# A fused attention and mixture-of-experts kernel: part of a weight conversion moved into the first expert, low parts of weights moved from GpSimd to VectorE

## The chip, the cores and the metric

One core of a Trainium2 chip. The metric is the device time of one execution, in microseconds. Engines: PE (TensorE), DVE (VectorE), ACT (ScalarE), POOL (GpSimd), SP (SyncE, which issues most of the loads here).

## What is computed

The reference, cut to what matters (x comes from the attention below; shapes in brackets):

```python
# attention with decay: B=4, H=8, S=768, D=64
state = gamma * state + einsum('bhd,bhe->bhde', k[:, :, t], v[:, :, t])
y[:, :, t] = scale * einsum('bhd,bhde->bhe', q[:, :, t], state)
# routing: x [3072, 512], w_gate [512, 8]; each expert takes 384 tokens
order = argsort(-(x @ w_gate).flatten())     # greedy, by falling logit
# experts: w1 [8, 512, 1024], w2 [8, 1024, 512]
out[mask_e] = maximum(x[mask_e] @ w1[e], 0) @ w2[e]
# dense block: w_in [512, 2048], w_out [2048, 512], both given in float64
h = x @ w_in
result = (maximum(h, 0) + log1p(exp(-abs(h)))) @ w_out
```

## The kernel before, in words

**Stages.** (1) Attention over 24 blocks of 128 tokens (class Attn), with the conversion of w_in and w_out laid beside it. (2) A gap in which only the routing of the first expert runs (Route.phase(0)). (3) Eight experts one after the other (class Ffn): for each, its 384 tokens are gathered from DRAM, go through w1, relu, w2 (steps M1 and M2, eight each), and then at once through the dense block (steps F1 and F2, sixteen each, on the same 384 columns); the rows are stored by an indirect DMA. The routing of the next expert runs beside the steps.

**Precision.** Every product of the experts is three matmuls in fp32r: high by high, low by high, high by low (mm3, lines 617 to 621). So every weight and every activation is split into a rounded high part (ACT, a copy into fp32r) and a low part, the difference. For weights this is split_w (lines 599 to 606): whi on ACT, wlo on POOL; w1, w2 and the rows of w_out are split each time they are used, 256 times in all. w_in is kept split (wih, wil). For activations it is split_act and split_g (lines 608 to 615, 688 to 698), low parts on DVE.

**Conversion.** w_in and w_out come as float64. Class Conv turns a piece of 128x512 into float32 with integer and float operations on DVE and one on ACT (line 240): operations m (line 233), cX (241), x (244), cX (247), e (251), F (260), and for w_in the low part (254). It is a generator: each yield is one step, and step() runs one. A piece of w_in takes seven, one of w_out six. It works on two pieces at once and loads raw pieces ahead (line 227). Attn.emit calls side(j, part) three times per block, which brings the steps done up to (3j + part) * 190 // 72: 187 of 208 by the end. The other 21 are run by fill() (line 833), one at each plain yield of Route.phase(0).

**Routing.** One phase picks one expert and its 384 tokens. top() finds each token's best expert still open, then a search in three levels counts tokens over thresholds: on DVE thr and G (compare, line 378), on PE 24 small matmuls (count, line 385), on DVE ind (431), on PE a sum over partitions (437), on DVE satj and base (440, 446). Then the expert is chosen (inc to ei, lines 466 to 474, mark "expert"), and its list of tokens is made (one-hots ohq, line 511; 24 matmuls, line 524; ix, line 529, mark "list"). Each yield ends a turn; what follows a yield is written to the queues later, after other work.

**Order.** All queues are in program order (manual_schedule). Ffn.plan lists the steps M1, M2, F1, F2 and transposes; Ffn.emit walks it. Before each step, weights(at + 4) makes sure that the split weights of the next four keys are written (ring of 6 pairs) and that raw loads are out ahead of them (4 buffers); then the step; then one turn of routing, at each step until the next expert's list is there, at every second step after that. Before F1 number 10 the next list is forced and its rows are gathered by POOL (fetch_x). fetch_w waits on SP for the number of the chosen expert.

Of the kernel before, what the change touches and what calls it, by code (L numbers as in the profile page):

```python
# [206 lines left out]
class Conv:  # L207
# [3 lines left out]
    def __init__(self, tc, ctx, W, plan):  # L211
        self.nc, self.W, self.plan = tc.nc, W, plan
        self.st = ctx.enter_context(tc.tile_pool(name="cst", bufs=2, side="right"))
        self.raw, self.loaded, self.ops = {}, 0, 0
        self.gen = self.run()

    def load(self, p):
        raw = self.raw[p] = self.st.tile([128, self.W, 2], I32, name="raw", bufs=3)
        self.nc.sync.dma_start(raw.rearrange("p n b -> p (n b)"), self.plan[p][0])

    def run(self):
# [4 lines left out]
        for p in range(N + 2):  # L226
            while self.loaded < min(p + 2, N):
                self.load(self.loaded)
                self.loaded += 1
# [27 lines left out]
            if b:  # L257
                to = self.plan[q][1]
                F = to[0] if len(to) == 1 else T("cF", FT, 2)
                v.tensor_tensor(F, m, e, op=OP.add)  # L260
                if len(to) == 2:
                    f = F.rearrange("p (a n) -> p a n", a=4)
                    nc.scalar.activation(to[0], f, AF.Copy)
                    c = f, to[1], to[0]
                yield
            b = a

    def step(self, to=None):

        while to is None or self.ops < to:  # L270
            self.ops += 1
            if next(self.gen, self) is self or to is None:
                return

# [6 lines left out]
class Route:  # L281
# [72 lines left out]
    def top(self, c0, c1, first):  # L354
# [5 lines left out]
        if not first:  # L360
            v.tensor_tensor(lm, src, self.pen[:, None, :].to_broadcast([128, n, E]), op=OP.add)
            src = lm
            v.tensor_scalar(self.u[:, s], self.asg[:, s], 0.0, None, op0=OP.is_equal)
        v.tensor_reduce(m, src, axis=AX.X, op=OP.max)
# [4 lines left out]
        v.tensor_reduce(aed, lm, axis=AX.X, op=OP.max)  # L369
        v.tensor_tensor(ik, m.bitcast(I32), sg, op=OP.bitwise_xor)  # L370
# [17 lines left out]
    def first_part(self, c0, c1):  # L388

        self.top(c0, c1, True)  # L390
        self.compare(c0, c1, self.t0, 46)

    def phase(self, i, slow=True):
# [5 lines left out]
        if i:  # L399
            self.top(0, N, False)  # L400
# [107 lines left out]
        h = N // 4  # L508
# [58 lines left out]
class Ffn:  # L567
# [7 lines left out]
    def open0(self, ctx):  # L575
        P = lambda name, bufs: ctx.enter_context(self.tc.tile_pool(name=name, bufs=bufs, reuse_waits="tile"))
        self.rawp = P("raw", 4)
        self.ring = P("ring", 6)
# [9 lines left out]
    def load_raw(self, key):  # L588
# [3 lines left out]
        raw = self.raws[key] = self.rawp.tile([128, 512], FT, name="wraw")  # L592
# [6 lines left out]
    def split_w(self, key):  # L599
        nc = self.nc  # L600
        raw = self.wout[key[2]] if key[0] == "wo" else self.raws.pop(key)
# [3 lines left out]
        nc.gpsimd.tensor_sub(lo, raw, hi.bitcast(FT))  # L605
# [161 lines left out]
    def emit(self):  # L767
# [9 lines left out]
        for n, (fn, i, f, key) in enumerate(G):  # L777
# [5 lines left out]
            fn(i, f)  # L783
            step += 1
# [3 lines left out]
    def weights(self, to):  # L788

        keys = self.keys  # L790
        while self.done < min(len(keys), to) and self.can(keys[self.done]):
            while self.loaded < min(len(keys), self.done + 4) and self.can(keys[self.loaded]):
                self.load_raw(keys[self.loaded])
                self.loaded += 1
# [21 lines left out]
    def start(self, fill):  # L816
# [5 lines left out]
        for mark in self.R.phase(0, False):  # L822
            self.marked(mark, 0)
            if mark == "expert":
                for k in self.keys[:4]:
# [6 lines left out]
            elif mark is None:  # L832
                fill()
# [10 lines left out]
def model(ctx, tc, qk, kv, w_gate, w1, w2, w_in, w_out, tab, gqt, out, B, H, S):  # L844
# [18 lines left out]
    cuts += [(w_out[f * 128:(f + 1) * 128], (wo[:, f],)) for f in range(16)]  # L863
# [3 lines left out]
    def side(j, part):  # L867
        cv.step((3 * j + part) * 190 // 72)
# [5 lines left out]
    a.emit(side, logits)  # L874
    c2.close()
    R.wp = ctx.enter_context(tc.tile_pool(name="rwork", bufs=1, reuse_waits="tile"))
# [3 lines left out]
    F.start(cv.step)  # L880
    cv.step(1000)
    c1.close()
    c0.close()
    F.open(ctx)
# [27 lines left out]
```

## Time and profile before

| | us |
|---|---|
| median of three runs | 1120.59 |
| the three runs | 1120.57, 1120.59, 1124.83 |
| the profiled execution | 1123.62 |
| its span, first to last instruction | 1121.5 |

| engine | busy us (share of the span) |
|---|---|
| PE | 1020.8 (91%) |
| DVE | 689.1 (61%) |
| ACT | 535.1 (48%) |
| POOL | 442.3 (39%) |

The shares are means over stages that differ: attention ends near 175 us, the first matmul of the first expert starts at 216.6, each expert takes 102 to 126 us. The mean granted TensorE clock is 0.957 of full speed. Matmuls are pipelined and their ends are modelled, so a busy PE in the tables need not be at its peak. Neighbouring operations of one engine overlap a little in the records, so sums of durations are some per cent above the busy time.

### The profile page before, as it was taken

What the parts mean: (1) busy time and instruction counts of PE and PEld (TensorE: products, weight loads), DVE (VectorE), ACT (ScalarE), POOL (GpSimd) and SP (SyncE); (2) the same over time, 40 slices, a digit from 0 to 9 for tenths busy, and PEclk for the clock granted to TensorE, in tenths of its full rate; (3) what the DMA queues carried; (4) which work ended last, traced back from release to release, by engine and by line L of the source; (5) the groups of instructions that cost most, each with busy time, mean ns of one, the idle gap of its engine ahead of it and who ended that gap; (6) DMA issues with size and microseconds to landing.
All of it is one profiled execution on the core that took longest, in us unless ns stands there. A gap on an engine that the chain in (4) does not pass through costs nothing.

```text
span 1121.5 us, 18513 instructions
## 1 busy us (share of the span) xinstructions
PE 1020.8 (91%) x7041; PEld 922.8 (82%) x7041; DVE 689.1 (61%) x1510; ACT 535.1 (48%) x1041; POOL 442.3 (39%) x386
## 2 busy tenths in 40 slices
PE   5877874489999999999999999999999999999997
PEld 5776763378878988898889888988888899989996
DVE  5999999755765656467646665865586622441332
ACT  2444332224554465436543654365536654664663
POOL 4323320333335424542355235523452454337422
PEclk9888886589999999999999999999999999999999
DMA  8887873320113201320122012301220222013000
GB/s 317 302 284 263 301 228 104 104 75 1 39 38 105 65 1 38 95 75 1 39 81 90 1 38 76 94 1 30 75 67 1 76 85 85 1 47 122 1 1 29
DMA packets 38873, 97.51 MB, mean 87 GB/s; under 512 B 5120, under 2 KB 5248, under 8 KB 38784
## 3 DMA queue, kind: packets, MB, share of 16 engines
q1 hardware_dynamic: 34128, 83.11, 23.1%
q0 software_dynamic: 3840, 12.59, 3.4%
q8 instruction: 55, 0.90, 0.3%
q10 hardware_dynamic: 816, 0.63, 0.2%
q14 instruction: 34, 0.28, 0.1%
HBM read 83.73 MB, written 12.58 MB: 86 GB/s over the span
## 4 chain that ended last, share of the span: by engine, by line
PE 68%; DVE 23%; issue 3%; ACT 2%; DMA 2%; POOL 1%; SPq 0%; ACTq 0%; POOLq 0%; DVEq 0%
PE h L619 11%; PE h L621 10%; PE h L620 10%; PE acc L717 8%; PE acc L719 7%; PE acc L718 7%; PE acc L619 3%; PE acc L621 3%; PE acc L620 3%; PE rt L385 2%; DVE at L121 2%; DVE cM L233 2%; DVE cX L247 2%; DVE cX L251 2%; DVE base L446 1%
## 5 line engine op out<-in xcount | busy, mean ns | idle before, releaser
L605 POOL TENSOR_TENSOR wlo<-wo,whi 128x512 fp32r<-128x512 f32 x128 | 169.2, 1327 | 357.9 <-ACT whi L604 325.4
L605 POOL TENSOR_TENSOR wlo<-wraw,whi 128x512 fp32r<-128x512 f32 x128 | 164.1, 1302 | 189.6 <-ACT whi L604 172.3
L683 DVE SCALAR_TENSOR_TENSOR gf<-h,sp 128x384 f32<-128x384 f32 x128 | 71.2, 557 | 179.0 <-ACT sp L681 178.9
L619 PE MATMUL h<-x2h,wih 128*128 128x384 f32 x512 | 176.8, 345 | 0.0
L621 PE MATMUL h<-x2l,wih 128*128 128x384 f32 x512 | 173.2, 338 | 0.2 <-DVE x2l L615 0.2
L620 PE MATMUL h<-x2h,wil 128*128 128x384 f32 x512 | 173.4, 339 | 0.0
L717 PE MATMUL acc<-whi,gh 128*128 128x512 f32 x384 | 154.8, 403 | 0.0
L719 PE MATMUL acc<-whi,gl 128*128 128x512 f32 x384 | 152.5, 397 | 2.2 <-DVE gl L697 2.2
L718 PE MATMUL acc<-wlo,gh 128*128 128x512 f32 x384 | 152.0, 396 | 0.0
L679 ACT ACTIVATE sp<-h 128x384 f32<-128x384 f32 x128 | 62.4, 488 | 150.3 <-PE h L621 148.9
L697 DVE TENSOR_TENSOR gl<-gf,gh 128x384 fp32r<-128x384 f32 x128 | 103.4, 807 | 39.9 <-ACT gh L696 39.8
L611 ACT ACTIVATE h1h<-h 128x384 fp32r<-128x384 f32 x64 | 31.4, 491 | 170.7 <-PE h L621 170.7
L612 DVE SCALAR_TENSOR_TENSOR h1l<-h,h1h 128x384 fp32r<-128x384 f32 x64 | 35.3, 555 | 115.6 <-ACT h1h L611 115.6
L619 PEld LDWEIGHTS h<-x2h,wih 128*128 128x128 f32 x512 | 96.1, 188 | 4.1
L620 PEld LDWEIGHTS h<-x2h,wil 128*128 128x128 f32 x512 | 96.2, 188 | 3.0
L621 PEld LDWEIGHTS h<-x2l,wih 128*128 128x128 f32 x512 | 96.1, 188 | 0.8 <-DVE x2l L615 0.8
L619 PE MATMUL acc<-h1h,whi 128*128 128x384 f32 x256 | 89.7, 350 | 0.0
L719 PEld LDWEIGHTS acc<-whi,gl 128*128 128x128 f32 x384 | 72.4, 189 | 21.0 <-DVE gl L697 4.3
L619 PE MATMUL h<-xh,whi 128*128 128x384 f32 x256 | 89.0, 348 | 0.7 <-ACT xh L614 0.7
L696 ACT ACTIVATE gh<-gf 128x384 fp32r<-128x384 f32 x128 | 67.1, 524 | 46.5 <-DVE gf L683 39.0
L621 PE MATMUL acc<-h1l,whi 128*128 128x384 f32 x256 | 87.4, 341 | 0.0
L620 PE MATMUL acc<-h1h,wlo 128*128 128x384 f32 x256 | 87.2, 341 | 0.0
(197 smaller groups left out, 2047.4 us busy)
## 6 DMA issues: line engine op xcount, KB each, us to landing
wraw<-in_moe_w_dram SPq DMA_DIRECT2D x128, 256.0 KB, 2.7
qk_t<-in_qk_dram SPq DMA_DIRECT2D x24, 512.0 KB, 6.8
kv_t<-in_kv_dram SPq DMA_DIRECT2D x24, 512.0 KB, 5.5
raw<-in_moe_w_in_dram SPq DMA_DIRECT2D x16, 512.0 KB, 5.3
raw<-in_moe_w_out_dram SPq DMA_DIRECT2D x16, 512.0 KB, 4.7
xd<-xs SPq DMA_DIRECT2D x24, 256.0 KB, 6.0
gqt<-in_gqt_dram SPq DMA_DIRECT2D x5, 256.0 KB, 6.6
ctab<-in_tab_dram ACTq DMA_DIRECT2D x1, 536.0 KB, 5.7
```

The lines of the kernel that those rows point to most:

```text
L605: nc.gpsimd.tensor_sub(lo, raw, hi.bitcast(FT))
L612: nc.vector.scalar_tensor_tensor(lo, ps, 0.0, hi.bitcast(FT), op0=OP.max, op1=OP.subtract)
L619: nc.tensor.matmul(ps, wh, ah, start=start, stop=False)
L620: nc.tensor.matmul(ps, wl, ah, start=False, stop=False)
L621: nc.tensor.matmul(ps, wh, al, start=False, stop=stop)
L679: nc.scalar.activation(a, ps, AF.Abs)
L683: nc.vector.scalar_tensor_tensor(g, ps, 0.0, a, op0=OP.max, op1=OP.add)
L696: nc.scalar.activation(gh, g, AF.Copy)
L697: nc.vector.tensor_tensor(gl, g, gh.bitcast(FT), op=OP.subtract)
L717: nc.tensor.matmul(ps, gh[:, s], wh, start=f == 0, stop=False)
L718: nc.tensor.matmul(ps, gh[:, s], wl, start=False, stop=False)
L719: nc.tensor.matmul(ps, gl[:, s], wh, start=False, stop=f == 15)
```

## The change

- Conv gets a number of raw buffers (bufs), counts the pieces it has made, and can be run until a given piece is done (until).
- In attention only w_in and the first 8 of the 16 rows of w_out are converted: 160 steps, spread so that the last call of side has done them all. Nothing of it is left for the gap: fill is gone.
- The other 8 rows are converted in the first expert, by a second Conv with pieces of 128x256 (16 of them, 96 steps): after each step of the plan with i == 0, three steps of it. split_w of a row of w_out first makes sure that its pieces are there.
- wlo is made on DVE (tensor_tensor) instead of POOL, in all 256 splits.
- A routing phase after the first has three more yields, two inside top() and one behind it.
- The ring has 5 pairs in place of 6, the raw weights 3 buffers in place of 4.

Cut to the changed lines and their neighbours:

```diff
@@ -208,14 +208,14 @@
-    def __init__(self, tc, ctx, W, plan):
-        self.nc, self.W, self.plan = tc.nc, W, plan
+    def __init__(self, tc, ctx, W, plan, bufs=3):
+        self.nc, self.W, self.plan, self.bufs = tc.nc, W, plan, bufs
         self.st = ctx.enter_context(tc.tile_pool(name="cst", bufs=2, side="right"))
-        self.raw, self.loaded, self.ops = {}, 0, 0
+        self.raw, self.loaded, self.ops, self.made = {}, 0, 0, 0
         self.gen = self.run()
     def load(self, p):
-        raw = self.raw[p] = self.st.tile([128, self.W, 2], I32, name="raw", bufs=3)
+        raw = self.raw[p] = self.st.tile([128, self.W, 2], I32, name="raw", bufs=self.bufs)
         self.nc.sync.dma_start(raw.rearrange("p n b -> p (n b)"), self.plan[p][0])
@@ -224,7 +224,7 @@
         for p in range(N + 2):
-            while self.loaded < min(p + 2, N):
+            while self.loaded < min(p + self.bufs - 1, N):
                 self.load(self.loaded)
@@ -262,6 +262,7 @@
                     c = f, to[1], to[0]
+                self.made += 1
                 yield
@@ -271,6 +272,10 @@
+    def until(self, made):
+        while self.made < min(made, len(self.plan)):
+            self.step()
@@ -361,12 +366,15 @@
             v.tensor_scalar(self.u[:, s], self.asg[:, s], 0.0, None, op0=OP.is_equal)
+            yield
         v.tensor_reduce(m, src, axis=AX.X, op=OP.max)
         v.tensor_reduce(aed, lm, axis=AX.X, op=OP.max)
+        if not first:
+            yield
         v.tensor_tensor(ik, m.bitcast(I32), sg, op=OP.bitwise_xor)
@@ -387,7 +395,8 @@
-        self.top(c0, c1, True)
+        for _ in self.top(c0, c1, True):
+            pass
         self.compare(c0, c1, self.t0, 46)
@@ -397,7 +406,8 @@
         if i:
-            self.top(0, N, False)
+            yield from self.top(0, N, False)
+            yield
         base = self.zero
@@ -575,7 +585,7 @@
         self.rawp = P("raw", 4)
-        self.ring = P("ring", 6)
+        self.ring = P("ring", 5)
@@ -589,7 +599,7 @@
             return
-        raw = self.raws[key] = self.rawp.tile([128, 512], FT, name="wraw")
+        raw = self.raws[key] = self.rawp.tile([128, 512], FT, name="wraw", bufs=3)
         e = bass.ds(self.regs[i], 1)
@@ -598,11 +608,13 @@
         nc = self.nc
+        if key[0] == "wo":
+            self.late.until(2 * (key[2] + 1 - self.kept))
         raw = self.wout[key[2]] if key[0] == "wo" else self.raws.pop(key)
         nc.scalar.activation(hi, raw, AF.Copy)
-        nc.gpsimd.tensor_sub(lo, raw, hi.bitcast(FT))
+        nc.vector.tensor_tensor(lo, raw, hi.bitcast(FT), op=OP.subtract)
         self.ws[key] = hi, lo
@@ -781,6 +793,9 @@
             fn(i, f)
+            if i == 0:
+                for _ in range(3):
+                    self.late.step()
             step += 1
@@ -789,7 +804,7 @@
         while self.done < min(len(keys), to) and self.can(keys[self.done]):
-            while self.loaded < min(len(keys), self.done + 4) and self.can(keys[self.loaded]):
+            while self.loaded < min(len(keys), self.done + 3) and self.can(keys[self.loaded]):
                 self.load_raw(keys[self.loaded])
@@ -813,7 +828,7 @@
-    def start(self, fill):
+    def start(self):
@@ -822,7 +837,7 @@
             if mark == "expert":
-                for k in self.keys[:4]:
+                for k in self.keys[:3]:
                     self.load_raw(k)
@@ -830,7 +845,6 @@
             elif mark is None:
-                fill()
                 if since is not None:
@@ -860,27 +874,32 @@
     cuts = [(w_in[f], (wih[:, :, f * 128:(f + 1) * 128], wil[:, :, f * 128:(f + 1) * 128])) for f in range(16)]
-    cuts += [(w_out[f * 128:(f + 1) * 128], (wo[:, f],)) for f in range(16)]
+    kept = 8
+    rows = [w_out[f * 128:(f + 1) * 128] for f in range(16)]
+    cuts += [(rows[f], (wo[:, f],)) for f in range(kept)]
     cv = Conv(tc, c1, 512, cuts)
     def side(j, part):
-        cv.step((3 * j + part) * 190 // 72)
+        cv.step((3 * j + part) * 162 // 71)
     a.emit(side, logits)
+    cv.step(1000)
     c2.close()
+    c1.close()
     R.wp = ctx.enter_context(tc.tile_pool(name="rwork", bufs=1, reuse_waits="tile"))
     F.open0(ctx)
-    F.start(cv.step)
-    cv.step(1000)
-    c1.close()
+    F.start()
     c0.close()
+    halves = [(rows[f][:, h * 512:h * 512 + 512], (wo[:, f, h * 256:h * 256 + 256],))
+              for f in range(kept, 16) for h in range(2)]
+    F.late, F.kept = Conv(tc, ctx, 256, halves, 3), kept
     F.open(ctx)
```

## Rows read from the trace of the kernel before

**Rows 1.** The page's chain of work that ended last, by engine, as shares of the span.
```profile
PE 68%; DVE 23%; issue 3%; ACT 2%; DMA 2%; POOL 1%; SPq 0%; ACTq 0%; POOLq 0%; DVEq 0%
```

**Rows 2.** Busy time of each engine by stage, us from the span's start: length, then PE, PEld (weight load), DVE, ACT, POOL busy us with instruction counts, the granted TensorE clock, the DMA engines' share and GB/s. Attention; the routing gap; a part of the gap with nearly the whole first routing phase; the first expert up to its first F1; the rest of the first expert; the later experts with routing beside them; an expert without.
```profile
18.00:175.50 157.50, 119.44 (x1370) 108.39 (x1370) 156.53 (x291) 66.07 (x131) 48.23 (x35) 0.88 0.81 272
175.50:216.60 41.10, 11.83 (x177) 9.00 (x173) 37.85 (x132) 6.80 (x11) 8.12 (x7) 0.55 0.36 107
178.30:211.30 33.00, 8.10 (x155) 6.50 (x154) 31.20 (x115) 3.86 (x6) 4.95 (x5) 0.52 0.26 82
216.60:268.30 51.70, 44.77 (x318) 41.48 (x318) 27.48 (x61) 13.24 (x27) 19.18 (x15) 0.86 0.14 43
268.30:335.50 67.20, 64.47 (x403) 56.83 (x403) 45.09 (x112) 37.16 (x73) 20.47 (x16) 0.97 0.11 32
335.50:907.50 572.00, 563.88 (x3606) 505.83 (x3606) 350.89 (x797) 294.02 (x573) 244.63 (x206) 1.00 0.17 52
907.50:1009.50 102.00, 102.00 (x542) 95.43 (x541) 33.54 (x49) 58.08 (x113) 47.09 (x41) 1.00 0.19 57
```

**Rows 3.** DVE's groups of instructions in attention (18 to 175.5 us), the six operations of a w_out piece: line, operation, tiles and shapes, count, busy us, mean ns of one, idle us before.
```profile
L233 DVE SCALAR_TENSOR_TENSOR cM<-cM,cX 128x512 f32<-128x512 f32 x29 | 24.8, 856 | 0.1
L247 DVE SCALAR_TENSOR_TENSOR cX<-raw,cX 128x512 int32<-128x512 int32 x29 | 21.8, 752 | 0.0
L251 DVE SCALAR_TENSOR_TENSOR cX<-raw,cX 128x512 f32<-128x512 uint32 x28 | 20.9, 747 | 0.0
L241 DVE TENSOR_SCALAR cX<-raw 128x512 int32<-128x512 int32 x29 | 16.6, 574 | 4.5 <-DMA raw<-in_moe_w_in_dram 4.5
L244 DVE TENSOR_SCALAR cX<-cM 128x512 int32<-128x512 int32 x28 | 15.5, 554 | 0.0
...
L260 DVE TENSOR_TENSOR wo<-cM,cX 128x512 f32<-128x512 f32 x12 | 10.8, 899 | 0.3
```

**Rows 4.** PE's groups in the same window, the one it waits before (idle us before it and what ended that).
```profile
L159 PE MATMUL pX<-rx,yT 128*128 128x136 f32 x184 | 32.2, 325 | 33.2 <-ACT yT L137 25.1 <-DVE cX L251 8.1
```

**Rows 5.** The timeline in the routing gap, one counting step of the first routing phase with the conversion steps beside it: start us, duration us, engine, line, operation, tiles; in brackets the engine's idle time before and what ended it.
```profile
186.53 1.08 PE L385 MATMUL pS<-G,oe 128*8 128x46 bf16 x24 [1.18 <-DVE G L378]
...
186.75 0.42 DVE L244 TENSOR_SCALAR cX<-cM 128x512 int32<-128x512 int32 x1
187.08 0.68 DVE L247 SCALAR_TENSOR_TENSOR cX<-raw,cX 128x512 int32<-128x512 int32 x1
...
187.68 0.25 DVE L431 TENSOR_SCALAR ind<-pS,r 8x46 bf16<-8x46 f32 x1
187.86 0.67 DVE L251 SCALAR_TENSOR_TENSOR cX<-raw,cX 128x512 f32<-128x512 uint32 x1
187.99 0.19 PE L437 MATMUL pS<-ind,ones 8*128 8x46 bf16 x1 [0.38 <-DVE ind L431]
...
188.46 0.19 DVE L440 SCALAR_TENSOR_TENSOR satj<-pS,st 128x46 bf16<-128x46 f32 x1
```

**Rows 6.** The same timeline from the first expert's choice to the making of its list.
```profile
196.33 0.17 PE L464 MATMUL pS<-rs,ones 128*128 128x8 bf16 x1 [1.82 <-DVE rs L457]
...
197.08 0.69 DVE L233 SCALAR_TENSOR_TENSOR cM<-cM,cX 128x512 f32<-128x512 f32 x1
197.68 0.16 DVE L466 TENSOR_TENSOR inc<-pS,rem 128x8 f32<-128x8 f32 x1
...
202.47 0.56 DVE L511 TENSOR_TENSOR ohq<-io,px 128x768 bf16<-128x768 bf16 x1
...
203.32 2.56 POOL L605 TENSOR_TENSOR wlo<-wraw,whi 128x512 fp32r<-128x512 f32 x2 [42.20 <-ACT whi L604]
203.39 1.36 DVE L517 TENSOR_TENSOR rh<-dd,cidb 128x144 bf16<-128x144 f32 x1
...
204.67 2.56 DVE L511 TENSOR_TENSOR ohq<-io,px 128x768 bf16<-128x768 bf16 x3
```

**Rows 7.** The timeline in the fifth expert, with three low parts of weights on POOL.
```profile
697.42 3.78 POOL L605 TENSOR_TENSOR wlo<-wraw,whi 128x512 fp32r<-128x512 f32 x3
...
697.54 3.68 DVE L446 TENSOR_TENSOR base<-ksat 128x1 f32<-128x1 f32 x1
...
700.60 0.10 PEld L464 LDWEIGHTS <-ones 128*128 128x128 bf16 x1 [0.16 <-issue]
```

**Rows 8.** The groups of the low parts on POOL (w_out's rows, then w1 and w2), of the high parts on ACT, and the page's row of the raw weights' loads (count, KB each, median us from issue to landing).
```profile
L605 POOL TENSOR_TENSOR wlo<-wo,whi 128x512 fp32r<-128x512 f32 x128 | 169.2, 1327 | 357.9 <-ACT whi L604 325.4
L605 POOL TENSOR_TENSOR wlo<-wraw,whi 128x512 fp32r<-128x512 f32 x128 | 164.1, 1302 | 189.6 <-ACT whi L604 172.3
...
L604 ACT ACTIVATE whi<-wraw 128x512 fp32r<-128x512 f32 x128 | 75.5, 623 | 18.2 <-DMA wraw<-in_moe_w_dram 16.0 <-POOL wlo L605 2.0
...
wraw<-in_moe_w_dram SPq DMA_DIRECT2D x128, 256.0 KB, 2.7
```

**Rows 9.** The page's groups of two low parts of activations on DVE: gl with both inputs in SBUF, h1l with one in PSUM.
```profile
L697 DVE TENSOR_TENSOR gl<-gf,gh 128x384 fp32r<-128x384 f32 x128 | 103.4, 807 | 39.9 <-ACT gh L696 39.8
...
L612 DVE SCALAR_TENSOR_TENSOR h1l<-h,h1h 128x384 fp32r<-128x384 f32 x64 | 35.3, 555 | 115.6 <-ACT h1h L611 115.6
```

**Rows 10.** The timeline at the second routing phase's first count, in the first expert: an early operation of its top part, and PE's count.
```profile
222.05 1.27 DVE L363 TENSOR_SCALAR unas<-asg 128x24 f32<-128x24 f32 x1
...
229.87 1.08 PE L385 MATMUL rt<-G,oe 128*8 128x46 bf16 x24 [4.88 <-DVE G L378]
```

## The prediction

> **What bounds the kernel now.** I read the chain of waits first, then the stages by window, then in each stage the engine that never rests.
>
> The chain gives 68% to PE and 23% to DVE [rows 1]; the windows place them [rows 2]. In attention (18 to 175.5 us) DVE is busy 156.5 of 157.5 us while PE is busy 119.4: DVE sets the pace, and most of what it does there is converting weights [rows 3]. From 175.5 to 216.6 us PE is busy 11.8 us and DVE 37.9: the first routing phase, one long chain through DVE with conversion steps laid between. From 216.6 us on PE sets the pace, unevenly: in an expert with no routing beside it (907.5 to 1009.5) it never idles; from 335.5 to 907.5 it idles 572.0 - 563.9 = 8.1 us, in the first expert (two windows) 6.9 + 2.7 = 9.6 us.
>
> Why PE idles there is seen in one spot: POOL runs three wlo back to back (3.78 us from 697.42), a one-element DVE operation takes 3.68 us from 697.54 on, and PE's next routing step starts only at 700.60 [rows 7]. With POOL quiet a whole 128x512 piece takes 0.68 [rows 5]. At the first routing phase of the experts a 24-column operation takes 1.27 us and PE waits 4.88 us for G behind such operations [rows 10]. gl, both inputs in SBUF, takes 807 ns at 384 columns; h1l, one input in PSUM, takes 555 [rows 9]. So in this trace much of DVE's time in the experts is waiting on POOL's wlo.
>
> **The change, part by part.**
>
> *Attention: 187 conversion steps become 160.* Removed are 27 w_out steps, 4.5 pieces of six. One of each kind, by the means in that window, is 0.856 + 0.752 + 0.747 + 0.574 + 0.554 + 0.899 = 4.38 us per piece [rows 3]; 4.5 of them are 19.7 us, less about 0.06 us per step by which neighbours overlap: 18 us. That is the upper bound. With POOL quiet a step takes 0.33 us (cX, 186.75 to 187.08) or 0.60 (187.08 to 187.68) from start to start [rows 5], and with two short and four long ones a piece is 3.06 us: 13.8 us for 4.5. POOL's own two products per iteration stay, so what collides with them stays, and I take the lower price. PE may not follow all the way: its 119.4 busy us would be 83% of 143.7, and it already waits 33.2 us ahead of pX, mostly for ACT's yT [rows 4]. That is late because ACT's queue also holds conversion steps that wait for DVE, so a lighter DVE frees it too; I leave 1 us for it. Term: **-13 us**, ends -4 (PE or the loads take over) and -18. The loads: eight pieces of 512 KB fewer in attention, hidden either way at a DMA share of 0.81 [rows 2].
>
> *Routing gap: 21 steps removed.* Start to start they are some 10.7 us of DVE, but they fill waits. Two steps at 186.75 and 187.08 end at 187.68, and PE's count ends at 186.53 + 1.08 = 187.61: removing them gains 0.07. The single step at 187.86 holds satj until 188.46, while PE ended at 188.18: 0.28 [rows 5]. The last two before inc hold it to 197.68, while PE ended at 196.33 + 0.17: 1.1 us or more [rows 6]. Reading all fourteen places so, the sum is 4.2 us. Then the low parts: on POOL (from 203.32) they collide with rh, 1.36 us, and three ohq, 2.56; one ohq ahead of them took 0.56, and rh is the smaller [rows 6]: about 1.0 us lost in each. On DVE two of them at 0.60 stand in the same chain and wait for whi, some 1.5 us. The gap shrinks by 4.2 + 2.0 - 1.5 = **4.6 us**; ends -2 and -8. The first gathers behind it now find POOL empty; they did so before.
>
> *Low parts on DVE.* 256 operations at 128x512, two inputs in SBUF, as a long conversion step: 0.60 us start to start with POOL quiet, 0.68 busy [rows 5]. That adds about 154 us to DVE over the experts and takes 333 us (169.2 + 164.1) off POOL [rows 8]. DVE's own work shrinks with it: gl from 0.81 towards 0.56, the stretched small operations from 1.2 to about 0.2 (inc 0.16, [rows 6]). In the experts with routing DVE is busy 350.9 of 572 us now; adding 5 x 32 x 0.6 = 96 us and taking away at least 20 leaves 75% or less, so PE is not slowed on average. In order, lo stands behind whi, which ACT does right after h1h, while DVE does h1l (0.56, [rows 9]) and the routing turn: whi (0.62, [rows 8]) is done before DVE arrives. Cost taken: nothing on the path, because each pair is made four weights ahead (some 8 us); if that cover goes, it is rival C. What it releases is PE's idle time in the later experts, 8.1 us plus a little of the clock: I take **-6**, ends 0 and -10.
>
> *First expert: 96 half-width steps, three per step of the plan, for 32 steps.* No such row exists. From 128x384 to 128x512 an operation falls by about 0.13 us per 128 columns (h1l 0.555, a long step 0.68), so at 256 it takes about 0.42, start to start 0.34, and the short kind 0.2: a mean of 0.29, 28 us in all. Bounds: half of 0.51 (24 us) and no saving from the width (49 us). Beside it come about 23 lo (14 us), h1l, x2l, gf and gl (14 us) and most of a routing phase. For that I take the gap: 31.2 busy us from 178.3 to 211.3 [rows 2], less some 12.5 of conversion, plus 2.5 for the top part: about 22 us, of which 19 fall in the 32 steps. DVE has 75 us to do; PE has 32 groups at 2.1 us (the expert without routing runs 48 in 102 us, [rows 2]) and 5 to 11 us of routing (a routed expert takes 113): 73 to 78. This is level, so some waits must stay. The kernel before loses 9.6 us of idling here and a few at half clock: the clock is 0.86 in the first window [rows 2]. The added turns (in top) let PE go on with weights where it waits 4.88 us now. I take **-7**, ends +6 and -13.
>
> *Three more turns per routing phase.* By count, the list of a phase is reached at the 32nd turn, and the first expert has 34 before its gather is forced, so nothing is drained in a hurry. Cost nothing; later phases end some 60 us later, in time in which PE has work.
>
> *Shallower buffers.* Raw weights 4 to 3 and the ring 6 to 5: a load lands in 2.7 us [rows 8] and has two weights (4 us) ahead of need; SP can be held by a late conversion load whose buffer DVE frees a step later. Cost nothing; without that cover ACT waits on raw weights, up to 1 us a weight in the first 16 steps; it is in the end +6 above.
>
> Sum: 13 + 4.6 + 6 + 7 = 30.6 us. The profiled execution took 1123.6 us (span 1121.5 and 2.1 around it): 1093.0. It is 3.0 us above the median of the three runs, 1120.6, so against that: **1090.0**.
>
> **The rivals.**
>
> A. *Attention is handed over*: PE, with its half-clock stretches (mean 0.88) and in-order waits, holds each iteration near its present length, and only 4 us come off. For it: PE's 33.2 us of waits [rows 4] lie on another engine too. Against: DVE never rests. Time: 1090 + 9 = 1099.
>
> B. *DVE becomes the bound in the first expert*, and the later ones give little: the two terms of the experts, -13, become 0. For it: my 75 us against 73 to 78 leaves no room for order. Against: today's stalls are of another kind. Time: 1103. The Trainium skill, Perfetto Trace Analysis, section Optimizing Scalar/DVE Operations, speaks for this one: where DVE is saturated, it suggests giving work away, to ScalarE or even GPSIMD, and this change does the reverse. By that rule the outcome is this rival's; the same section doubts that moving work between those two engines helps, and rows 7 show why.
>
> C. *Head of the line on DVE, slower than before.* POOL now idles 325.4 + 172.3 us until whi is ready [rows 8], 1.9 us for each of 256, and only its own transfers stand behind it. On DVE the routing chain and the next h1l would. DVE has 572.0 - 350.9 us free over five experts, 44 in each; lo takes 19 of them and the shorter waits give about as much back, so 1.4 us are free for each of 32 lo: from there each further 0.1 us costs PE 3.2 us per expert, 22 us over seven. A wait of 1.6 us costs 45 us against 30 gained: 1135. Against: the waits on POOL are those of an engine that came early with nothing else to do.
>
> D. *All bounds reached*: attention -18, gap -6, PE's idling in the experts nearly all gone, -20: 1077.
>
> That the change doesn't do what it says could be if the late half were forced out in a block ahead of the second weight's first use. Three turns a step make 84 of 96 by the 28th step, where 12 are needed, so I give that nothing.
>
> **How the numbers follow.** Forecast 0.62, A 0.12, B 0.13, C 0.06, D 0.07. About 0.5%, 5.6 us, is what a measurement of this kernel can tell from no change. The forecast's own ends (attention -8 to -17, gap -3 to -6, experts -6 to -18) give 1079 to 1104; the range of 8 in 10 takes in A and B and D's edge: 1077 to 1107. C lies outside, and so does D's far half. Faster by over 0.5%: 0.89, nearly all of the cases but C and a bad end of B; within: 0.05; slower: 0.06.
>
> **What would show it.** Attention's last chunk should end near 162 us, with DVE still busy above 95% of it (below 90%: A). The gap should be near 36 us. POOL should hold only gathers and stores in the experts; gl should be near 0.55 us and no small DVE operation over 0.5; lo should be near 0.69. PE should idle under 3 us in the second to sixth experts. In the first expert DVE should be above 85% until the late half is done, and PE's idling there should be 3 to 8 us. Wrong it would be if lo showed waits for whi of over a microsecond on the average (C), or if the first expert's two windows took as long as now, 118.9 us (B).

## The result, and the profile after

The changed kernel takes 1094.8 us (median of four runs, 1092.2 to 1095.45) against 1120.6: a ratio of 0.976 (95% interval 0.973 to 0.978). The forecast was 1090.0, with a range of 1077 to 1107. The profiled execution is the fastest run, 1092.2 us, with a span of 1090.4; that of the kernel before lay 3.0 us above its median. So the two spans differ by 31.1 us and the two medians by 25.8. Chain, then stages (columns as in [rows 2]: attention, gap, first expert in two parts, second to sixth experts, seventh):

```profile
PE 68%; DVE 16%; issue 10%; DMA 3%; ACT 2%; POOL 1%; SPq 0%; ACTq 0%; POOLq 0%; DVEq 0%
```

```profile
18.00:162.40 144.40, 113.10 (x1370) 102.46 (x1370) 141.66 (x270) 64.14 (x127) 55.44 (x35) 0.92 0.80 276
162.40:201.00 38.60, 11.48 (x173) 9.13 (x173) 25.10 (x109) 4.31 (x7) 3.06 (x3) 0.53 0.30 96
201.00:243.00 42.00, 40.87 (x293) 38.26 (x293) 36.19 (x108) 16.76 (x35) 0.00 (x0) 0.94 0.32 100
243.00:315.70 72.70, 69.67 (x434) 61.17 (x434) 60.02 (x186) 44.42 (x91) 3.22 (x4) 1.00 0.18 52
315.70:874.90 559.20, 556.16 (x3577) 500.27 (x3577) 342.06 (x959) 291.06 (x565) 32.32 (x45) 1.00 0.17 52
874.90:978.00 103.10, 103.10 (x565) 96.42 (x564) 47.33 (x83) 58.36 (x113) 6.28 (x9) 1.00 0.19 59
```

The chain's shares are not to be set against [rows 1]: its "issue" is almost all one piece of 91.6 us in the last expert, between two stores of POOL, in which PE is busy throughout. For the stages, the kernel before cut at the same instructions (first expert; second to sixth):

```profile
216.60:342.30 125.70, 116.04 (x751) 104.03 (x752) 76.58 (x184) 54.53 (x107) 40.94 (x32) 0.93 0.13 37
342.30:907.50 565.20, 557.08 (x3574) 500.10 (x3573) 346.87 (x786) 289.88 (x565) 243.33 (x205) 1.00 0.17 52
```

DVE still fills attention (141.7 of 144.4 us). In the first expert it is busy 36.2 of the 42.0 us up to the first F1, where it was busy 27.5 of 51.7 [rows 2], and PE idles 1.1 + 3.0 us in the whole of it in place of 9.7. POOL is all but empty. In the second to sixth experts PE idles 3.0 us in place of 8.1, and DVE takes less time (342.1 us) for 959 operations than it took for 786 before (346.9).

The table gives the time between starts of instructions, in us: the last L of attention (the operation that writes tile L, line 162), the first list (ix), the first M1 matmul of each expert (h<-xh,whi).

| | before | after | difference | forecast |
|---|---|---|---|---|
| start to the last L | 175.4 | 161.3 | -14.1 | -13 |
| last L to the list | 32.4 | 27.8 | -4.6 | -4.6 (whole gap) |
| list to the first M1 | 8.8 | 11.9 | +3.1 | 0 |
| first expert | 125.7 | 114.7 | -11.0 | -7 |
| second to sixth experts | 565.2 | 559.1 | -6.1 | -6 |
| seventh | 101.9 | 103.1 | +1.2 | 0 |
| eighth, to the end | 112.1 | 112.4 | +0.3 | 0 |
| span | 1121.5 | 1090.4 | -31.1 | -30.6 |

The seventh expert's 1.2 us is no wait: PE never idles there, but has 565 instructions in place of 542 [rows 2], since a list of 24 matmuls now falls there. In the same way one count of 24 has moved out of the first expert (725 in place of 751), which is a part of its gain.

DVE in attention, the kinds of [rows 3]:

```profile
L247 DVE SCALAR_TENSOR_TENSOR cX<-raw,cX 128x512 int32<-128x512 int32 x24 | 21.1, 881 | 0.0
L251 DVE SCALAR_TENSOR_TENSOR cX<-raw,cX 128x512 f32<-128x512 uint32 x24 | 21.1, 881 | 0.0
L233 DVE SCALAR_TENSOR_TENSOR cM<-cM,cX 128x512 f32<-128x512 f32 x24 | 17.4, 726 | 0.1
...
L244 DVE TENSOR_SCALAR cX<-cM 128x512 int32<-128x512 int32 x24 | 13.2, 550 | 0.0
L241 DVE TENSOR_SCALAR cX<-raw 128x512 int32<-128x512 int32 x24 | 13.2, 549 | 4.7 <-DMA raw<-in_moe_w_in_dram 4.7
...
L260 DVE TENSOR_TENSOR wo<-cM,cX 128x512 f32<-128x512 f32 x8 | 5.5, 689 | 0.2
```

There are 24 pieces now. One operation of each kind comes to 4.28 us, hardly less than the 4.38 before [rows 3], and POOL, with its own products, is still busy 55.4 us in this stretch.

The gap, to be read against [rows 5] and [rows 6]; then the first transpose in it:

```profile
165.56 1.07 PE L393 MATMUL pS<-G,oe 128*8 128x46 bf16 x24 [1.07 <-DVE G L386]
...
166.67 0.25 DVE L441 TENSOR_SCALAR ind<-pS,r 8x46 bf16<-8x46 f32 x1 [0.81 <-PE pS L393]
...
167.20 0.20 DVE L450 SCALAR_TENSOR_TENSOR satj<-pS,st 128x46 bf16<-128x46 f32 x1 [0.28 <-PE pS L447]
...
185.27 0.31 DVE L527 TENSOR_TENSOR rh<-dd,cidb 128x144 bf16<-128x144 f32 x1
185.60 1.52 DVE L617 TENSOR_TENSOR wlo<-wraw,whi 128x512 fp32r<-128x512 f32 x2
...
187.04 1.49 DVE L521 TENSOR_TENSOR ohq<-io,px 128x768 bf16<-128x768 bf16 x3
...
189.14 0.16 DVE L539 SCALAR_TENSOR_TENSOR ix<-pS,ix 128x3 int32<-128x3 f32 x1
...
190.26 1.16 POOL L643 DMA_INDIRECT rows<-xd,ix  x1 [41.94 <-DVE wlo L617]
190.32 1.38 SPq L219 DMA_DIRECT2D raw<-in_moe_w_out_dram  x3
```

```profile
196.14 1.11 PE L654 MATMUL h<-identp,rows 128*128 128x128 f32 x4 [2.41 <-DMA rows<-xd,ix]
```

After the change DVE waits for PE (idle 0.81 us ahead of ind), where [rows 5] had two conversion steps: nothing gained there, as costed. rh takes 0.31 us, three ohq 1.49, and two wlo 1.52 with their wait. The list is 4.6 us sooner. But then three late raw loads of 256 KB leave SP at 190.32, between the first gather and the second, and the first transpose starts 5.9 us after the first gather. Before, it was 3.6:

```profile
207.84 0.16 DVE L529 SCALAR_TENSOR_TENSOR ix<-pS,ix 128x3 int32<-128x3 f32 x1
...
208.30 1.16 POOL L631 DMA_INDIRECT rows<-xd,ix  x1 [2.42 <-DVE ix L529]
...
211.91 1.11 PE L642 MATMUL h<-identp,rows 128*128 128x128 f32 x4 [1.28 <-DMA rows<-xd,ix]
```

The low parts on DVE (page groups; idle before, and its releaser), and gl and base in the second to sixth experts, to be read against [rows 8], [rows 9] and [rows 7]:

```profile
L617 DVE TENSOR_TENSOR wlo<-wraw,whi 128x512 fp32r<-128x512 f32 x128 | 86.0, 685 | 6.3 <-ACT whi L616 6.1
...
L617 DVE TENSOR_TENSOR wlo<-wo,whi 128x512 fp32r<-128x512 f32 x128 | 87.2, 685 | 0.9 <-ACT whi L616 0.9
```

```profile
L709 DVE TENSOR_TENSOR gl<-gf,gh 128x384 fp32r<-128x384 f32 x80 | 44.1, 552 | 6.2 <-ACT gh L708 6.2
...
L456 DVE TENSOR_TENSOR base<-ksat 128x1 f32<-128x1 f32 x15 | 2.4, 160 | 0.5
```

### The profile page after: what moved, and what is told of

Same layout as the page of the kernel before. It is cut to its first block, busy times and chain, and to the rows that moved or that the text cites. A ratio compares the mean times of both kernels' runs of the same rounds, so it can differ in the third digit from the quotient of the medians.

```text
span 1090.4 us, 18474 instructions
## 1 busy us (share of the span) xinstructions
PE 1008.5 (92%) x7041; PEld 913.3 (84%) x7041; DVE 702.9 (64%) x1814; ACT 539.1 (49%) x1049; POOL 115.3 (11%) x130
## 4 chain that ended last, share of the span: by engine, by line
PE 68%; DVE 16%; issue 10%; DMA 3%; ACT 2%; POOL 1%; SPq 0%; ACTq 0%; POOLq 0%; DVEq 0%
PE h L631 11%; PE h L633 10%; PE h L632 10%; PE acc L729 7%; PE acc L731 7%; PE acc L730 7%; PE acc L631 3%; PE acc L633 3%; PE acc L632 3%; PE rt L393 2%; DVE at L121 2%; DVE cX L247 2%; DVE cX L251 2%; DVE cM L233 1%; DMA raw<-in_moe_w_in_dram 1%
## 5 line engine op out<-in xcount | busy, mean ns | idle before, releaser
L623 ACT ACTIVATE h1h<-h 128x384 fp32r<-128x384 f32 x64 | 31.5, 492 | 155.7 <-PE h L633 149.6
L616 ACT ACTIVATE whi<-wraw 128x512 fp32r<-128x512 f32 x128 | 76.4, 623 | 33.9 <-DMA wraw<-in_moe_w_dram 33.6
L617 DVE TENSOR_TENSOR wlo<-wraw,whi 128x512 fp32r<-128x512 f32 x128 | 86.0, 685 | 6.3 <-ACT whi L616 6.1
L617 DVE TENSOR_TENSOR wlo<-wo,whi 128x512 fp32r<-128x512 f32 x128 | 87.2, 685 | 0.9 <-ACT whi L616 0.9
L632 PE MATMUL h<-xh,wlo 128*128 128x384 f32 x256 | 87.2, 341 | 0.0
L633 PE MATMUL h<-xl,whi 128*128 128x384 f32 x256 | 87.2, 341 | 0.0
```

Source lines behind the costliest of these rows:

```text
L616: nc.scalar.activation(hi, raw, AF.Copy)
L617: nc.vector.tensor_tensor(lo, raw, hi.bitcast(FT), op=OP.subtract)
L623: nc.scalar.activation(hi, ps, AF.Relu)
L632: nc.tensor.matmul(ps, wl, ah, start=False, stop=False)
L633: nc.tensor.matmul(ps, wh, al, start=False, stop=stop)
```

## The experiments

Stages as in the table above, each from one profile; totals are medians of four to six runs, beside which the kernel before took 1121.1 to 1123.5. Attention carries noise: eight kernels with the same 160 steps have the last L between 160.5 and 166.5 us, mean 162.8; three with 187 steps between 174.6 and 175.5.

| run | total | last L | to the list | to the first M1 | first expert | 2nd to 6th | 7th |
|---|---|---|---|---|---|---|---|
| e1_lo_on_pool | 1103.1 | 162.0 | 28.5 | 9.3 | 122.4 | 564.0 | 103.1 |
| e2_before_lo_on_dve | 1101.5 | 174.6 | 31.5 | 9.5 | 111.9 | 556.5 | 101.9 |
| e3_before_lo_memset | 1101.4 | 175.5 | 30.3 | 8.9 | 113.4 | 556.6 | 101.9 |
| e4_no_added_turns | 1096.5 | 163.0 | 27.8 | 11.9 | 120.6 | 556.5 | 101.9 |
| e5_twelve_rows_late | 1091.3 | 152.7 | 27.7 | 12.0 | 122.1 | 559.9 | 103.1 |
| e6_late_from_third_step | 1092.3 | 166.5 | 28.6 | 9.5 | 114.5 | 559.2 | 103.1 |
| e7_lo_twice | 1112.1 | 162.9 | 29.6 | 11.7 | 127.1 | 565.5 | 103.1 |
| e8_no_late_half | 1112.8 | 190.7 | 28.3 | 9.5 | 109.6 | 559.2 | 103.1 |
| e9_turns_in_phase_1_only | 1092.6 | 162.2 | 28.0 | 11.8 | 115.6 | 557.9 | 101.9 |
| e10_late_third_and_turns_1 | 1088.0 | 160.5 | 28.4 | 9.5 | 115.3 | 557.9 | 101.9 |
| e11_ten_rows_late | 1093.3 | 155.5 | 27.7 | 9.7 | 124.0 | 557.9 | 101.9 |
| e12_lo_on_pool_no_turns | 1119.0 | 163.6 | 28.5 | 9.1 | 135.7 | 565.7 | 101.9 |

**What do the low parts on DVE do?** In the changed kernel, back on POOL:

```diff
-        nc.vector.tensor_tensor(lo, raw, hi.bitcast(FT), op=OP.subtract)
+        nc.gpsimd.tensor_sub(lo, raw, hi.bitcast(FT))
```

> The changed kernel with the low parts of the weights back on POOL, all else as changed. Theory (POOL's low parts hold up DVE, and PE idles behind DVE): attention as in the changed kernel; the first expert, 125.7 us before and 114.7 after from its first M1 to the next expert's, goes to 123 to 135, since the late conversion now meets POOL too; the second to sixth, 565.2 before and 559.1 after, go to 563 to 567; total 1108 to 1120. Rival (the added turns and the shorter attention made the gain, the engine of the low parts does not matter): first expert at most 118, total under 1100.

The second to sixth experts come out as the theory has it (564.0), the first just short of its range (122.4). The total, 1103.1, is above the rival's and below the theory's range: 8.3 us more than the changed kernel. Part of what I left out is in the gap, where the list to the first M1 takes 9.3 us in place of 11.9 (explained below, with the gap). The kernel before with the reverse of this edit alone:

> The kernel before with only one thing changed: the low parts of the weights on DVE. Theory (collisions): attention as before; first expert 108 to 117 us (no late conversion there), second to sixth 558 to 562, the gap within 1 us of before; total 1101 to 1107. Rival (DVE is filled up by the low parts and the gain in the experts comes from elsewhere): first expert 122 or more, total 1116 or more.

1101.5 us, ratio 0.980 (0.978 to 0.983): on the kernel before, this edit alone gives 2.0%, where the whole change gives 2.4. The second to sixth experts, 556.5, fall further than I expected. Its first expert:

```profile
215.60:327.50 111.90, 109.74 (x752) 98.13 (x753) 71.51 (x213) 54.76 (x107) 2.92 (x4) 1.00 0.14 39
```

PE's work there is that of the kernel before (752 and 751 instructions). Of the 13.8 us gained, 7.5 are idle time of PE (9.7 to 2.2), and 6.3 are busy time (116.0 to 109.7), at a mean granted clock of 1.00 in place of 0.93.

Whether PE waited for POOL itself, its low parts being late, the trace before answers: PE is in no wait that a wlo ended. Nearly all its idle time from the first to the sixth expert is spent waiting for DVE: 11.1 us before counts (for G), 3.6 for rs, 2.2 for gl. [rows 7] show no such wait yet, for the weight load at 700.60 had waited 0.16 us. It comes three DVE operations (gx, gg, rs) after the stretched base:

```profile
702.39 0.17 PE L464 MATMUL rt<-rs,ones 128*128 128x8 bf16 x1 [1.63 <-DVE rs L457]
```

The kernel before with POOL writing in place of reading:

```diff
-        nc.gpsimd.tensor_sub(lo, raw, hi.bitcast(FT))
+        nc.gpsimd.memset(lo.bitcast(FT), 0.0)
+        nc.gpsimd.memset(lo.bitcast(FT), 0.0)
```

> The kernel before with POOL writing zeros twice into each low part in place of the subtraction: about the same number of us on POOL, but it reads nothing from SBUF; the low parts of the weights are left out by this. Theory (it is POOL's reads that collide with DVE operations of two inputs in SBUF): gl falls from 807 ns to about 550, base from 1.1 us to 0.2, and the experts fall nearly as with the low parts on DVE, total 1100 to 1108; operations of one input (unas, thr) may stay long if they collide with writes. The Trainium skill, SBUF - State Buffer, section Who interferes with whom, states the first and allows the second. Rival (any work of POOL holds up DVE, or PE waits for POOL's own lateness): gl stays near 800 ns, total 1114 or more.

1101.4 us, in the theory's range and the same as with the low parts on DVE, though POOL works 2 x 0.53 us for each low part. First the stage of the second to sixth experts, then DVE and POOL groups from 342 to 908 us of this run, then three of the same DVE groups in the kernel before, and thr in the changed kernel (315.7 to 874.9 us):

```profile
328.10:884.70 556.60, 555.05 (x3575) 500.21 (x3574) 249.81 (x786) 290.60 (x565) 198.68 (x366) 1.00 0.17 53
```

```profile
L698 DVE TENSOR_TENSOR gl<-gf,gh 128x384 fp32r<-128x384 f32 x80 | 44.3, 554 | 20.5 <-ACT gh L697 19.8
...
L422 DVE TENSOR_SCALAR thr<-thrA,ksat 128x46 f16<-128x46 f32 (+1 forms) x13 | 5.4, 414 | 0.5
...
L446 DVE TENSOR_TENSOR base<-ksat 128x1 f32<-128x1 f32 x14 | 2.2, 160 | 0.5
...
L363 DVE TENSOR_SCALAR unas<-asg 128x24 f32<-128x24 f32 x5 | 0.9, 172 | 0.0
```

```profile
L606 POOL MEMSET wlo<- 128x512 f32 x169 | 89.3, 528 | 9.7
L605 POOL MEMSET wlo<- 128x512 f32 x169 | 89.2, 528 | 314.1 <-PE acc L719 250.3 <-PE acc L621 35.9 <-PE h L621 27.9
```

```profile
L697 DVE TENSOR_TENSOR gl<-gf,gh 128x384 fp32r<-128x384 f32 x80 | 60.6, 758 | 19.0 <-ACT gh L696 18.9
...
L446 DVE TENSOR_TENSOR base<-ksat 128x1 f32<-128x1 f32 x14 | 17.9, 1282 | 0.5
L422 DVE TENSOR_SCALAR thr<-thrA,ksat 128x46 f16<-128x46 f32 (+1 forms) x14 | 14.2, 1012 | 0.5
```

```profile
L432 DVE TENSOR_SCALAR thr<-thrA,ksat 128x46 f16<-128x46 f32 (+1 forms) x15 | 3.7, 246 | 0.5
```

The same 786 operations of DVE take 249.8 us here and took 346.9 before: 97 us of what counted as busy was waiting. gl and base, of two inputs in SBUF, are as fast as in the changed kernel. Of one input, unas is healed as well (172 ns, 1.27 us in [rows 10]), but thr is still slowed: 241 to 247 ns with no memset beside it, 429 to 705 with one. So what held up DVE was POOL's reading of SBUF, and for thr, though not for unas, its writing does it too. The Trainium skill, SBUF — State Buffer, section Who interferes with whom, has this rule (a DVE instruction with two inputs in SBUF collides with a GpSimd instruction that reads SBUF, not with one that only writes), and the trace agrees for gl and base.

Does lo wait at the head of DVE's queue (rival C), and how much room has DVE? Every lo made twice:

```diff
+        nc.vector.tensor_tensor(lo, raw, hi.bitcast(FT), op=OP.subtract)
         nc.vector.tensor_tensor(lo, raw, hi.bitcast(FT), op=OP.subtract)
```

> The changed kernel with every low part of a weight made twice on DVE: 256 more operations of 0.6 us, 154 us of DVE. Theory (from the second expert on DVE has some 44 us free in each, so another 19 us find room; in the first it has none): second to sixth experts 559.1 plus 0 to 8, the last two within 1 us, first expert 114.7 plus 9 to 16; total 1104 to 1118. Rival (the low parts stand at the head of DVE's queue and PE pays for each): second to sixth longer by 25 us or more, total over 1130.

```profile
204.10:331.20 127.10, 115.67 (x725) 103.53 (x726) 115.43 (x322) 60.90 (x125) 3.13 (x4) 0.94 0.20 63
331.20:896.70 565.50, 559.68 (x3576) 503.15 (x3576) 447.87 (x1119) 291.67 (x565) 33.77 (x45) 0.99 0.17 52
```

The second to sixth experts take 6.4 us more for 160 more operations, 0.04 us each: there DVE has room. The first takes 12.4 us more for its 29 (20.1 us of DVE): there DVE, busy 115.4 of 127.1 us, has room for little of it. All stages and the total lie in the theory's ranges. In the changed kernel all waits of lo for whi come to 7.0 us (6.1 + 0.9 above), 0.03 us for each of 256. Rival C is out.

**What do the turns do?** Without the three yields:

```diff
             v.tensor_scalar(self.u[:, s], self.asg[:, s], 0.0, None, op0=OP.is_equal)
-            yield
...
-        if not first:
+        if False:
             yield
...
             yield from self.top(0, N, False)
-            yield
```

> The changed kernel without the three added turns per routing phase. Theory (they only let PE go on with weights while DVE does the top part): first expert 0 to 4 us longer than 114.7, the later ones within 2 us of 559.1 in all, total 1094 to 1100. Rival (the turns are a main part of the gain in the experts): first expert 120 or more, total over 1101.

The first expert is 5.9 us longer, past my 4 and where the rival puts it (120.6); the total is the theory's. The later ones are shorter, 2.6 us in the second to sixth, past my 2, and 1.2 in the seventh. So the turns are about half of the first expert's gain and cost 3.8 us after it. The edits of e4 and e1 together:

> The changed kernel with the low parts back on POOL and without the added turns, so that of its edits only the moved conversion and the shallower buffers are left. Theory (the turns cover part of what the collisions cost the first expert, so they were worth more with POOL than the 5.9 us that they are worth with DVE): first expert 129 to 140 against 122.4 with the turns; second to sixth 564 to 567; total 1108 to 1118. Rival (turns and collisions do not touch each other): first expert 127 to 129, total 1104 to 1108.

So in the first expert the turns are worth 135.7 - 122.4 = 13.3 us with the low parts on POOL and 5.9 on DVE: the gains of the two edits do not add there, as is to be expected if both heal the same waits. The total, 1119.0, is just past the range, the rest as the theory has it. The moved conversion with the shallower buffers, without these two edits, is thus worth 0.4% (ratio to before 0.996, 0.994 to 0.998). With the turns in one phase alone:

```diff
-            yield from self.top(0, N, False)
-            yield
+            for _ in self.top(0, N, False):
+                if i == 1:
+                    yield
+            if i == 1:
+                yield
```

> The changed kernel with the three added turns in the second routing phase alone (the one beside the first expert) and none in the six later ones. Theory (they help where DVE is full and cost the later experts 3.8 us): first expert 114 to 116, second to sixth 556 to 558, seventh 101.9; total 1090 to 1093. Rival (the later experts' 2.6 us are noise of the profile): total 1094 to 1096.

All as the theory has it: the later experts fall by 1.2 + 1.2 us, the first keeps its gain but 0.9, and part of that is the count of 24 matmuls, which is back in it (750 instructions of PE in place of 725). The other 1.4 us of the 2.6 stay, with the second phase's turns. What the turns cost is seen in the changed kernel's fifth expert:

```profile
693.96 1.49 DVE L521 TENSOR_TENSOR ohq<-io,px 128x768 bf16<-128x768 bf16 x3
...
695.37 0.68 DVE L617 TENSOR_TENSOR wlo<-wo,whi 128x512 fp32r<-128x512 f32 x1
...
695.97 1.48 DVE L627 TENSOR_TENSOR x2l<-acc,x2h 128x384 fp32r<-128x384 f32 x3
...
696.57 0.44 PE L633 MATMUL h<-x2l,wih 128*128 128x384 f32 x1 [1.20 <-DVE x2l L627]
```

x2l stands behind lo and the one-hots of a list that three turns have pushed to this place, and PE waits 1.20 us for it. The sixth expert has another such wait, 1.3 us; e4 has none in these experts. Together they are 2.5 of the 3.0 us that PE idles from the second to the sixth.

**What is late in the gap?** The late conversion begun two steps later:

```diff
-            if i == 0:
+            if i == 0 and step >= 2:
                 for _ in range(3):
                     self.late.step()
```

> The changed kernel with the late conversion begun at the third step of the plan in place of the first, so that its first three loads of 256 KB come after the gathers of the first expert's rows and not beside them. Theory (those loads delay the gathers): from the list (ix) to the first M1 takes 9 to 10 us in place of 11.9, first expert within 2 us, total 1091 to 1094. Rival (the gathers are late for another reason, such as the wait of POOL for a low part): 11 to 12 us as now, total 1094 to 1097.

```profile
195.06 0.16 DVE L539 SCALAR_TENSOR_TENSOR ix<-pS,ix 128x3 int32<-128x3 f32 x1
...
196.18 1.29 POOL L643 DMA_INDIRECT rows<-xd,ix  x1 [42.09 <-DVE wlo L617]
...
200.56 1.97 PE L654 MATMUL h<-identp,rows 128*128 128x128 f32 x8 [1.43 <-DMA rows<-xd,ix]
```

As the theory has it. From the first gather to the first transpose it takes 4.4 us in place of 5.9, from the list to the first M1 2.4 us less: the loads it was. e1 bears this out without moving them in the program. There, with lo on POOL, the same three loads stand on SP behind a load of a raw weight that leaves only as the first lo behind the gathers ends (195.25 + 1.28 us on POOL), 5.0 us after the first gather (191.55):

```profile
196.55 0.33 SPq L607 DMA_DIRECT2D wraw<-in_moe_w_dram  x1
197.00 1.42 SPq L219 DMA_DIRECT2D raw<-in_moe_w_out_dram  x3
```

So the delay needs both edits: the late conversion, and lo on DVE, where it no longer holds SP until POOL has gathered. The rest against before, 0.7 us, is open: the first gather leaves 1.1 us after the list in place of 0.5, and the trace puts that down to a lo on DVE, but with lo on POOL (e1) it is 1.0 us too.

**How much to convert where?** Four fewer rows in attention, and then eight more (kept = 16, and 210 in side):

```diff
-    kept = 8
+    kept = 4
...
-        cv.step((3 * j + part) * 162 // 71)
+        cv.step((3 * j + part) * 138 // 71)
```

> The changed kernel with 12 of the 16 rows of w_out converted in the first expert in place of 8 (24 steps fewer in attention, 136 in all; 48 half-width steps more in the first expert, 144 in 48 steps of the plan). Theory (DVE still sets attention's pace, at 0.5 to 0.67 us a step; the first expert's DVE is full): attention 12 to 16 us shorter, first expert 114.7 plus 4 to 12, the gap as it is; total 1085 to 1094. Rival (PE or the loads already set attention's pace): attention at most 6 us shorter, total 1094 or more.

> The changed kernel with all of w_out converted in attention (208 steps there, none in the first expert and none in the gap). Theory (48 steps at 0.5 to 0.67 us against an overfull first expert that pays 3 to 9 us for its half): attention 24 to 32 us longer, first expert 106 to 112, from the list to the first M1 9 us, total 1108 to 1120. Rival (attention has room beside the conversion, so that it costs little there): attention under 15 us longer, total under 1103.

By the last L, 136, 160 (mean), 187 (mean), 208 steps take 152.7, 162.8, 175.2, 190.7 us: a step costs 0.42 us, then 0.46, then 0.74. The first is under what I expected of e5 (8.6 us off attention against the changed kernel, not 12 to 16); its first expert and total are in the range, and e8 is as the theory has it. The late half costs the first expert 114.7 - 109.6 = 5.1 us and the gather 2.4, for 28 us of attention; the next four rows cost it 7.4, for 10.

**Together.** The edits of e6 and e9:

> The changed kernel with both edits that were tried alone: the late conversion from the third step on, the added turns in the second routing phase alone. Theory (the two gains lie in different stages and add): 9.5 us from the list to the first M1, second to sixth experts 556.5 to 558, seventh 101.9; total 1087 to 1091. Rival (what one gives the other takes, so the total stays that of either alone): 1091.5 to 1094.

1088.0 us (1086.5 to 1090.5), ratio to before 0.969 (0.967 to 0.972): in the stages the gains add (2.4 us in the gap, 1.2 and 1.2 in the later experts, less 0.6 in the first), and this version beats the changed kernel. They make 4.2 of the 6.8 us between the medians; the rest is not placed. With two more rows late (kept = 6, and 150 in side):

> The same with both edits and 10 rows of w_out in the first expert in place of 8: 148 steps in attention, 120 late ones in 40 steps of the plan. Theory (a step costs attention 0.4 to 0.5 us at this number, and a half-width step costs the first expert less than that until DVE is full): attention 4 to 6 us shorter, first expert 1 to 5 us longer; total 1085 to 1091. Rival (the first expert is full already): first expert longer by 6 or more, total above that of the same with 8 rows.

The rival holds: attention is 5.0 us shorter, the first expert 8.7 longer, and PE idles 10.1 us in it in place of 3.8. The longest such wait begins at 301.0, before the sum over partitions, until ind is made:

```profile
304.46 0.42 DVE L260 TENSOR_TENSOR wo<-cM,cX 128x256 f32<-128x256 f32 x1
304.80 0.25 DVE L444 TENSOR_SCALAR ind<-rt,r 8x46 bf16<-8x46 f32 x1
...
305.10 0.19 PE L450 MATMUL rt<-ind,ones 8*128 8x46 bf16 x1 [4.07 <-DVE ind L444]
```

On DVE ind stands behind six operations of the late conversion (302.43 to 304.88), which now reaches the steps in which the next expert's rows are transposed and a turn of the next routing comes at every step.

## Why the prediction was right, point by point

The total, 1094.8, lies 4.8 us above the forecast. That the two spans differ by just about the forecast's sum (31.1 and 30.6) is luck in two ways: attention differs by up to 6 us between kernels with the same steps, and errors of opposite sign met. The gap and the turns cost what I had put at nothing, and the first expert gave more than I asked of it.

- **Attention**, -13: -14.1 between the two profiles, -12.4 between the means of all kernels with 160 and 187 steps. The lower price per step was the right one, 0.46 us against my 0.51; PE did not take over (rival A out). That DVE stays the pace at 136 steps was not shown; the price falls there.
- **Gap**, -4.6 (its own terms add up to 4.7): right for the routing chain, and by parts. With the conversion steps taken out and lo left on POOL (e1) the list is 3.9 us sooner, where I had 4.2; with lo alone on DVE (e2) 0.9, where I had 0.5. It was wrong for the gap. The step that failed is "the first gathers behind it now find POOL empty; they did so before": I counted POOL's queue and not SP's, where the late conversion's first three loads go out beside the gathers. It cost 3.1 us, 2.4 of them shown by e6.
- **Low parts on DVE**, -6 in the second to sixth experts: -6.1 in the profile, but it is a sum of two: -8.7 from the low parts (e2) and +2.6 from the turns (e4). With lo alone on DVE (e2), or POOL writing only (e3), PE idles 1.5 us there, so most of the 8.1 came from the collisions, as I had it.
- **Three more turns, cost nothing**: wrong, by 3.8 us in the later experts (e4). "In which PE has work" is true of PE; but DVE's order changes, and x2l comes late (2.5 us); some of the rest is routing work that the turns moved there from the first expert.
- **First expert**, -7: -11.0. The mechanism held: DVE is full (86% in the first part) and PE idles 4.1 us, in the 3 to 8 that I had named. The size was low. Step by step: -13.8 from the low parts (e2), +8.7 for the late half without the turns (e4 against e2), -5.9 from the turns. What I sized wrongly is PE's busy time at the lower clock: I had "a few" us, and in e2 it falls by 6.3 for the same instructions, nearly as much as the idle time does. The work of the late half was estimated well: the two kinds of half-width operations take 0.42 and 0.28 us, and 0.34 and 0.20 from start to start. (The routing work beside it adds up to 21.2 us from the terms given, not 22.)
- **Rival B** did not come, but e5, e7 and e11 show its edge: the first expert grows by 7.4 us with four more rows, by 8.7 with two more on top of both later edits, and by 12.4 with 20 us more of low parts. The Trainium skill, Perfetto Trace Analysis, section Optimizing Scalar/DVE Operations, suggests taking work off a saturated DVE, and doubts that GpSimd helps as the taker. The doubt is what the trace agrees with: in e1, with lo given to POOL, the first expert is 7.7 us longer. Giving work to ScalarE was not tried.
- **Shallower buffers**: not tried alone. ACT's waits for raw weights rose from 16.0 to 33.6 us. The longest, in the gap, went from 11.0 to 22.8, the others in all from 5.0 to 10.8. What that costs, if anything, no run shows.

Open: why attention differs by up to 6 us between kernels with the same 160 steps. It may be most of the spread of the totals, which one trace per kernel can't show.

## What to carry to other kernels

Before an engine is called busy, compare the same operation with its neighbour engine quiet: a 0.16 us operation that takes 1.3 is waiting, and moving the other engine's work onto it can make it less loaded. Gains need not add: undo each edit in both surroundings, as with the turns here. When a load is moved, or the engine that frees its queue changes, look at which transfers it now leaves beside, queue by queue.

## What was not expected of the hardware

Two engines' work on the same number of us collided or not by what one of them reads: POOL's subtraction, 1.30 us, stretched base to a mean of 1282 ns, and POOL's two memsets, 1.06 us, left it at 160. And three loads of 256 KB issued beside three gathers put off the first transpose by 1.5 us and the first M1 by 2.4.
